# Row statistics of two tiles on ScalarE, one load for two tiles, an uneven split of the last tile and a reordered list in a fused attention and MLP kernel

## The chip, the cores and the metric

The kernel runs on one core of a Trainium2 chip. The time is device microseconds of one execution; a run of the kernel before took 220.25 us (median of 3, 219.59 to 220.25). Besides the times there is one profiled execution, from which all rows come.

## The reference

x has 2048 rows of 512 values in bf16. The result is the sum of x, an attention branch and an MLP branch, both fed by the layer norm of x:

```
xn = layernorm(x)                                    # over 512 columns, no scale or bias
q, k, v = xn @ wq, xn @ wk, xn @ wv                  # 32 heads of 16, 4 segments of 512 rows
for each segment s:
    p     = softmax(causal(q k^T / 4));  a_dot = p v
    a_mem = phi(q) M / (phi(q) z + 1e-6)             # phi(t) = t + 1 if t > 0 else exp(t)
    o     = sigmoid(beta) a_mem + (1 - sigmoid(beta)) a_dot
    M += phi(k)^T v;  z += sum of phi(k)
out = x + o @ wo + silu(xn @ w1) @ w2                # w1: 512 x 1792, w2: 1792 x 512
```

## The kernel before, in words

The 2048 rows are 16 tiles of 128, four to a segment. The whole order of the work is written out by hand in the string ORDER (line 17). Each word of it is one small piece of work: a letter code that names a function in the dictionary PIECES (line 867), and numbers for segment, tile and part. The loop at line 904 calls the pieces in this order; each engine and each queue then executes its own instructions in the order in which they were issued, and waits where an operand is not ready.

The words that matter here:

- `xc` and `xd` (ln_sums, ln_var, lines 284 and 288) take one bn_stats and one bn_aggr of a tile of x on VectorE; `xs` is both. `xq` (ln_sqrt, line 302) takes the square root of variance plus eps on ScalarE, `xi` (line 305) the reciprocal on VectorE, and `Nv` (ln_norm, line 313) normalises the tile on VectorE. From tile 4 on, `xg` takes the roots of four tiles on GpSimd instead.
- `X` (turn_mm, line 840) transposes a normalised tile with four products on TensorE, and `Xa` or `Xv` (turn_copy, line 847) copies it out of PSUM on ScalarE, in two halves, or on VectorE. From tile 4 on `XD` transposes by a DMA on SP's queue.
- `k`, `q`, `v`, `h` are the dense products of a segment, in four parts per group in segments 0 and 1 (each part one product of 512 columns or two of 256); `kv`, `ka`, `qv`, `qa`, `vv` are the copies out of PSUM, on VectorE or ScalarE; `kf` and `kp` split k for the scores; `ha` and `hv` are the tanh and the product of silu; `fa`, `fp`, `fv`, `ga` are pieces of phi; `tb` is a one-element exponential that brings its table in early; `tanh` is one small ScalarE step; `lw` loads w2 or wo on ScalarE's queue.
- `S` (scores, line 707) is one of 72 batches of scores: 8 or 16 small products into the one psS tile, which takes four PSUM banks (psatt, bufs=1), and one exponential over 128x2048 on ScalarE; GpSimd then masks it. `E` and `O` weigh v with them. The batches run in the list's order S0, S2, S1, S3, S4, S7, S5, S11, S6, S8, S9, S10, S13 and on to S71.
- `o`, `oc`, `od` (out_mm, line 628) are output products with all, half or a quarter of the 512 columns; `oh` (half_out, line 660) is the same for the last tile, which is made in two halves of 256 columns, h = 0 and 1. `st` (lines 616 and 674) evicts and stores a tile, `sh` (half_store, line 663) a half of the last one. Outputs of the last segment's tiles 2 and 3 lie in the banks of the psS tile.
- `busy` (line 861) issues products on zeros whose result nobody reads, 44 and then 6 at the start.

The four loads of the first tiles of x are issued at lines 163 to 166, tiles 0 and 2 on SP's queue, 1 and 3 on ScalarE's; SP then issues the weights wv, wk, wq, further x, and w1.

Late in the list TensorE's products are issued as four narrow ones of 32 output rows each (product, line 333), side by side in the array.

Of the kernel before, what the change touches and what calls it, by code (L numbers as in the profile page):

```python
# [8 lines left out]
AF = mybir.ActivationFunctionType  # L9
# [5 lines left out]

ORDER = """
ones0 ones1 zeros xc0 xd0 xc1 xq0 xi0 Nv0 busy44 xd1 xq1 xc2 busy6 xi1 X0.1 xd2 xq2 Nv1 X1.1 Xa0.1 v0.0.0 v0.0.1 v0.0.2 xs3 xi2 Nv2 xq3 xi3 v0.0.3 X2.1 Xa1.1 k0.1.0 tb Nv3 X3.1 Xv2.1 k0.1.1 Xv3.1 vv0.0 odd omask k0.0.0 k0.0.1 k0.0.2 k0.0.3 ka0.0 fp0.0 q0.0.0 kf0.0 q0.0.1 q0.0.2 q0.0.3 k0.1.2 k0.1.3 q0.2.0 v0.2.0 qa0.0 xs5 ka0.1 kp0.1
S0 v0.1.0 v0.1.1 xs6 xs7 q0.2.1 v0.2.1 v0.2.2 v0.2.3 vv0.2 fa0.0 k0.2.0 k0.2.1 k0.2.2 xs4 xg4.4
S2 q0.2.2 q0.2.3 qv0.2 k0.2.3 kv0.2 fa0.2 v0.1.2 v0.1.3 vv0.1 Nv5 Nv6 XD6 q0.1.0 q0.1.1 q0.1.2 q0.1.3 Nv7 qv0.1
S1 h0.0.0 h0.0.1 h0.0.2 fp0.2 xs10 h0.0.3 v0.3.0 v0.3.1 v0.3.2 v0.3.3 ha0.0 vv0.3 q0.3.0 hv0.0  # L20
S3 h0.3.0 h0.3.1 q0.3.1 kp0.2 q0.3.2 h0.3.2 tanh XD5 XD7 q0.3.3 h0.3.3 k0.3.0 qv0.3 k0.3.1 xs8 ha0.3
S4 Nv4 h0.1.0 k0.3.2 h0.1.1 hv0.3 XD4 h0.2.0 h0.2.1 h0.2.2 h0.2.3 ha0.2 xs9 k0.3.3 kv0.3 hv0.2
S7 xs11 xg8.4 v1.2.0 v1.2.1 v1.2.2 v1.2.3 vv1.2 h0.1.2 h0.1.3 ha0.1 E0
S5 h0.4.0 h0.4.1 hv0.1 Ev0 h0.4.2 h0.4.3 v1.1.0 v1.1.1 fv0.2 v1.1.2 v1.3.0 fp0.3 ha0.4 v1.1.3 vv1.1
S11 hv0.4 q1.2.0 q1.2.1 q1.2.2 v1.3.1 kind fa0.1 q1.2.3 qv1.2 v1.3.2 v1.3.3 vv1.3 Nv8 XD8 O0 lw0 fv0.0 Ov0
S6 fa0.3 k1.2.0 k1.2.1 k1.2.2 h0.5.0 h0.5.1 h0.5.2 q1.1.0 h0.5.3 ha0.5 kp0.3 k1.2.3 kv1.2 q1.1.1 q1.1.2 hv0.5
S8 h0.7.0 q1.1.3 qv1.1 h0.6.0 h0.6.1 h0.6.2 h0.6.3 ha0.6 kp1.2 fv0.3 E1 Ev1 k1.0.0
S9 hv0.6 h0.7.1 h0.7.2 h0.7.3 Om0 ha0.7 k1.0.1 k1.0.2 q1.0.0 q1.0.1 fp0.1 Nv9 XD9 k1.0.3 q1.0.2 kv1.0 kp1.0
S10 h0.8.0 hv0.7 xs12 h0.8.1 h0.8.2 h0.8.3 ha0.8 h0.9.0 h0.9.1 q1.0.3 t0.3 qv1.0 Nv10 XD10 h0.9.2 h0.9.3
S13 hv0.8 O1 Ov1 xs15 v1.0.0 v1.0.1 v1.0.2 ha0.9 v1.0.3 vv1.0 h0.10.0 h0.10.1 bmask  # L30
# [63 lines left out]
def kernel(  # L94
# [207 lines left out]
    def ln_sqrt(t):  # L302
        nc.scalar.activation(out=rstd_all[:, t, :], in_=mv_all[:, t, 1:2], func=AF.Sqrt, bias=eps[:, 0:1])

# [8 lines left out]
    def ln_norm(t, eng):  # L313
        xn[t] = work.tile([P, D], BF16, name="xn_t", tag="x_res", bufs=4)
        eng.tensor_scalar(  # L315
            out=xn[t][:], in0=xs(t, t + 1)[:, 0, :], scalar1=mv_all[:, t, 0:1], scalar2=rstd_all[:, t, 0:1],
            op0=ALU.subtract, op1=ALU.mult,
        )
# [344 lines left out]
    def half_store(h):  # L663

        st, j, cols = sts[LAST], TPS - 1, slice(h * D // 2, (h + 1) * D // 2)
        assert len(st.pop(("done", j, h))) == 4 * (FT + DT)
        o_half = work.tile([P, L], BF16, name="o_half", tag="pos")[:, 0 : D // 2]
        out = nc.vector.scalar_tensor_tensor(
            out=o_half, in0=st["psO", j, h], scalar=0.5, in1=st["x", j][:, cols], op0=ALU.mult, op1=ALU.add
        )  # L670
        fin_out.append(((j, h), out))
        nc.sync.dma_start(out=out_flat[(NT - 1) * P : NT * P, cols], in_=o_half)
# [188 lines left out]
    def keep_busy(n):  # L861
# [81 lines left out]
```

## Time and profile before

| | us |
|---|---|
| median of 3 runs | 220.25 |
| profiled execution | 219.92 |
| its span | 218.2 |
| TensorE busy | 210.5 |
| ScalarE busy | 184.2 |
| VectorE busy | 179.0 |
| GpSimd busy | 126.8 |

The span is counted from the first to the last event of the profiled execution; times such as 7.17 are microseconds from its start. In the rows, PE is TensorE (PEld its weight loads), ACT ScalarE, DVE VectorE, POOL GpSimd, SP the SyncE queue. A row of the order in time has the start, the time until the last instruction of the group ends, the engine, the source line, the operation, output <- input, and the count. A row of the table by stretches has the stretch, its length, the busy time and instruction count of PE, PEld, DVE, ACT and POOL, the clock granted to TensorE, the DMA share and GB/s. A row of the chain of waits has start, length, engine, output, source line and count.

### The profile page before, as it was taken

How to read it: one execution, taken by the hardware profiler on the slowest of the kernel's cores; microseconds unless marked ns; L12 is line 12 of the kernel's file. 1: busy time of each engine (PE TensorE's matmuls, PEld its weight loads, DVE VectorE, ACT ScalarE, POOL GpSimd, SP SyncE). 2: the span in 40 equal slices, each digit the busy share in tenths (PEclk: the TensorE clock that was granted, in tenths of full speed). 3: DMA queues.
4: the chain of work that ended last, by engine and by line, in shares of the span. 5: the costliest groups of instructions: out<-in, count | busy, mean ns of one | idle time of the engine just before them, and what ended most of it. 6: DMA issues, size and time to landing. Idle time of an engine off the chain costs nothing.

```text
span 218.2 us, 9261 instructions
## 1 busy us (share of the span) xinstructions
PE 210.5 (96%) x3979; PEld 115.0 (53%) x4003; DVE 179.0 (82%) x370; ACT 184.2 (84%) x173; POOL 126.8 (58%) x203
## 2 busy tenths in 40 slices
PE   7899999999999999999999999999999999999994
PEld 7566656655644544444444545445454544465663
DVE  5899999999799879557989886887878897868753
ACT  3799999999999999999999999999989998942000
POOL 6066868969568973886766436963786373410000
PEclk9999999999999999999999999999999999999999
DMA  5995348322203222442125131420042120412322
GB/s 179 357 373 152 51 110 258 62 66 53 51 5 99 75 63 39 99 79 52 49 70 81 54 96 28 74 74 9 0 131 76 48 75 13 133 34 80 91 77 75
DMA packets 33273, 19.60 MB, mean 90 GB/s; under 512 B 14672, under 2 KB 33232, under 8 KB 33232
## 3 DMA queue, kind: packets, MB, share of 16 engines
q1 hardware_dynamic: 30608, 16.39, 28.7%
q10 hardware_dynamic: 2624, 2.62, 3.8%
q8 instruction: 31, 0.51, 1.0%
q14 instruction: 10, 0.08, 0.1%
HBM read 9.96 MB, written 2.10 MB: 55 GB/s over the span
## 4 chain that ended last, share of the span: by engine, by line
PE 92%; DVE 2%; ACT 2%; DMA 1%; issue 1%
PE ps L336 26%; PE psO L338 16%; PE ps L338 16%; PE psS L724 11%; PE psO L336 9%; PE psV L791 8%; PE psS L338 4%; ACT Pb L730 2%; DMA x_lo<-in_A_x_dram 1%; DVE stats L286 1%; PE psM L452 1%; PE ptr L845 0%; DVE xn_t L315 0%; PE ps L509 0%; DVE odd L828 0%
## 5 line engine op out<-in xcount | busy, mean ns | idle before, releaser
L730 ACT ACTIVATE Pb<-psS 128x2048 bf16<-128x2048 f32 x72 | 135.2, 1878 | 4.5 <-PE psS L724 2.2
L744 POOL TENSOR_SCALAR_AFFINE_SELECT Pb<-Pb 128x512 bf16<-128x512 bf16 (+2 forms) x88 | 62.1, 715 | 22.1 <-ACT Pb L730 19.2
L497 DVE SCALAR_TENSOR_TENSOR hT<-th,ps 128x512 bf16<-128x512 bf16 x56 | 38.0, 682 | 11.0 <-ACT th L492 10.6
L744 POOL TENSOR_SCALAR_AFFINE_SELECT lows<-Pb 64x512 bf16<-64x512 bf16 (+1 forms) x40 | 22.9, 572 | 32.5 <-ACT Pb L730 24.2
L338 PE MATMUL psO<-w_sb,hT 128*32 128x512 bf16 (+2 forms) x692 | 41.0, 320 | 0.0
L336 PE MATMUL ps<-xnT,w_sb 128*128 128x512 bf16 (+1 forms) x177 | 36.1, 330 | 0.4 <-DVE pk L433 0.2
L492 ACT ACTIVATE th<-ps 128x512 bf16<-128x512 f32 x56 | 33.0, 593 | 3.7 <-PE ps L338 3.3
L338 PEld LDWEIGHTS <-hT 128*32 128x32 bf16 x860 | 21.4, 96 | 14.5 <-issue 3.1
L338 PE MATMUL ps<-xnT,w_sb 128*32 128x512 bf16 (+1 forms) x408 | 24.6, 349 | 0.0
L724 PE MATMUL psS<-qT,k 32*128 32x64 bf16 (+3 forms) x512 | 23.0, 233 | 0.2
L336 PEld LDWEIGHTS <-w_sb 128*128 128x128 bf16 x178 | 16.4, 98 | 12.0 <-issue 1.2
L336 PE MATMUL psO<-w_sb,hT 128*128 128x512 bf16 (+2 forms) x83 | 20.6, 325 | 0.6 <-issue 0.5
L791 PEld LDWEIGHTS <-Vz 128*32 128x32 bf16 x768 | 16.0, 97 | 9.5 <-issue 0.6
L791 PE MATMUL psV<-Pb,Vz 128*32 128x448 bf16 (+7 forms) x512 | 20.9, 286 | 0.0
L724 PEld LDWEIGHTS <-k 32*128 32x128 bf16 x512 | 9.3, 92 | 21.5 <-issue 20.3
L724 PE MATMUL psS<-qT,kT 16*128 16x448 bf16 (+3 forms) x256 | 14.7, 269 | 0.0
L336 PE MATMUL ps<-xnT,wk_sb 128*128 128x256 bf16 (+1 forms) x63 | 14.1, 326 | 0.2
L336 PEld LDWEIGHTS <-hT 128*128 128x128 bf16 x93 | 8.5, 98 | 9.7 <-issue 2.1
L338 PEld LDWEIGHTS <-w_sb 128*32 128x32 bf16 x408 | 9.9, 96 | 6.6 <-issue 1.5
L828 DVE CAST odd<-psV 128x512 bf16<-128x512 f32 x16 | 11.0, 686 | 2.6 <-PE psV L791 2.4
L399 DVE CAST qT<-ps 128x512 bf16<-128x512 f32 x15 | 10.3, 687 | 3.4 <-PE ps L336 1.8
L338 PE MATMUL psO<-wo_sb,oT 128*32 128x512 bf16 x140 | 12.8, 380 | 0.0
(112 smaller groups left out, 326.7 us busy)
## 6 DMA issues: line engine op xcount, KB each, us to landing
spr<-rz SPq DMA_DIRECT2D x56, 64.0 KB
x_res<-in_A_x_dram SPq DMA_DIRECT2D x16, 128.0 KB
out_dram<-o_out SPq DMA_DIRECT2D x15, 128.0 KB
w_sb<-in_B_w_dram SPq DMA_DIRECT2D x2, 896.0 KB
w_sb<-in_B_w_dram ACTq DMA_DIRECT2D x1, 1792.0 KB
x_hi<-in_A_x_dram SPq DMA_DIRECT2D x2, 512.0 KB
wv_sb<-in_A_wv_dram SPq DMA_DIRECT2D x2, 256.0 KB
wk_sb<-in_A_wk_dram SPq DMA_DIRECT2D x1, 512.0 KB
```

The lines of the kernel that those rows point to most:

```text
L286: nc.vector.bn_stats(out=stats[t][:], in_=xs(t, t + 1)[:, 0, :])
L336: return [nc.tensor.matmul(out, lhsT=lhsT, rhs=rhs, start=start, stop=stop, skip_group_check=True)]
L338: nc.tensor.matmul(out[c : c + 32], lhsT=lhsT[:, c : c + 32], rhs=rhs, start=start, stop=stop, tile_position=(0, c), skip_group_check=True,)
L399: copy(out=seg_tile(s, "qT")[:, dt, :], in_=sts[s].pop(("q", dt))[:, :])
L452: nc.tensor.matmul(psM[32 * g : 32 * g + 32, i, :].rearrange("p (r d) -> p r d", d=DH), lhsT=st["phiK", dt][:, j, 32 * g : 32 * g + 32], r ...
L492: nc.scalar.activation(out=th[:], in_=sts[s]["h", ft][:, :], func=AF.Tanh, scale=0.5)
L497: nc.vector.scalar_tensor_tensor(out=st["hT"][:, ft, :], in0=st.pop(("th", ft))[:], scalar=1.0, in1=st.pop(("h", ft))[:, :], op0=ALU.add, ...
L724: nc.tensor.matmul(psS[:, g, c : c + q2 - q1], lhsT=keys[rows], rhs=st["qT"][rows, dt, q1:q2], start=True, stop=True, tile_position=(32 * ...
L730: exp = nc.scalar.activation(out=blocks(Pb, b).rearrange("p y g c -> p g y c"), in_=psS[:, :, :].rearrange("p g (y c) -> p g y c", c=BLOCK ...
L744: over[id(Pb)].append(nc.gpsimd.affine_select(out=out, in_=in_, compare_op=ALU.is_ge, fill=0.0, base=base, pattern=[[0, out.shape[1]], [1, ...
L791: nc.tensor.matmul(psV[32 * g : 32 * g + 32, q0 : q0 + nq].rearrange("p (y c) -> p y c", y=weights.shape[2]), lhsT=Vzs[s % 2][:, kt, 4 * d ...
L828: copy(out=odd[:], in_=sts[s].pop(("psV", 1))[:, :])
```

## The change

Five things change.

1. Tiles 1 and 3 of x get their sums on ScalarE: `xa` takes the negative mean (Copy with scale -1/512 and accumulation), `xb` the sum of the squared deviations (Square with the negative mean as bias, and accumulation). The root then scales by 1/512 and the normalisation adds instead of subtracting. `xc1`, `xd1` and `xs3` go.
2. x's tiles 2 and 3 come in one load of 256 KB on ScalarE's queue, behind tile 1's; SP has one load fewer.
3. The idle products are 40 in one row instead of 44 and 6.
4. The turned tiles 0 and 1 are copied by VectorE in one piece each (`Xv`) instead of by ScalarE in two.
5. The last tile is made in parts of 128 (h = 0, stored last) and 384 columns (h = 1). The list is reordered: from the start to S10, in one word around S68 and S66, and in the last line.

```diff
-    load_x(nc.sync, 2, 1)
-    load_x(nc.scalar, 3, 1)
+    load_x(nc.scalar, 2, 2)
...
+    def ln_mean_act(t):
+        by_act.add(t)
+        nc.scalar.activation(
+            out=work.tile([P, D], BF16, name="junk", tag="ex")[:], in_=xs(t, t + 1)[:, 0, :],
+            func=AF.Copy, scale=-1.0 / D, accum_out=mv_all[:, t, 0:1],
+        )
+
+    def ln_square_act(t):
+        nc.scalar.activation(
+            out=work.tile([P, D], BF16, name="junk", tag="ex")[:], in_=xs(t, t + 1)[:, 0, :],
+            func=AF.Square, bias=mv_all[:, t, 0:1], accum_out=mv_all[:, t, 1:2],
+        )
...
-        width = D if half is None else D // 2
-        first = 0 if half is None else half * width
+        first, width = (0, D) if half is None else LAST_COLS[half]
...
+    LAST_COLS = [(0, P), (P, D - P)]
...
-        st, j, cols = sts[LAST], TPS - 1, slice(h * D // 2, (h + 1) * D // 2)
+        (first, width), st, j = LAST_COLS[h], sts[LAST], TPS - 1
+        cols = slice(first, first + width)
...
-        ptr, parts = xn.pop(("ptr", t)), 2 if t < 2 else 1
+        ptr, parts = xn.pop(("ptr", t)), 2 if t < 2 and copy is act else 1
```

The old list up to S3 and from S11 to S8 (lines 17 to 21 and 25 to 27):

```
ones0 ones1 zeros xc0 xd0 xc1 xq0 xi0 Nv0 busy44 xd1 xq1 xc2 busy6 xi1 X0.1 xd2 xq2 Nv1 X1.1 Xa0.1 v0.0.0 v0.0.1 v0.0.2 xs3 xi2 Nv2 xq3 xi3 v0.0.3 X2.1 Xa1.1 k0.1.0 tb Nv3 X3.1 Xv2.1 k0.1.1 Xv3.1 vv0.0 odd omask k0.0.0 k0.0.1 k0.0.2 k0.0.3 ka0.0 fp0.0 q0.0.0 kf0.0 q0.0.1 q0.0.2 q0.0.3 k0.1.2 k0.1.3 q0.2.0 v0.2.0 qa0.0 xs5 ka0.1 kp0.1
S0 v0.1.0 v0.1.1 xs6 xs7 q0.2.1 v0.2.1 v0.2.2 v0.2.3 vv0.2 fa0.0 k0.2.0 k0.2.1 k0.2.2 xs4 xg4.4
S2 q0.2.2 q0.2.3 qv0.2 k0.2.3 kv0.2 fa0.2 v0.1.2 v0.1.3 vv0.1 Nv5 Nv6 XD6 q0.1.0 q0.1.1 q0.1.2 q0.1.3 Nv7 qv0.1
S1 h0.0.0 h0.0.1 h0.0.2 fp0.2 xs10 h0.0.3 v0.3.0 v0.3.1 v0.3.2 v0.3.3 ha0.0 vv0.3 q0.3.0 hv0.0
S3 h0.3.0 h0.3.1 q0.3.1 kp0.2 q0.3.2 h0.3.2 tanh XD5 XD7 q0.3.3 h0.3.3 k0.3.0 qv0.3 k0.3.1 xs8 ha0.3
...
S11 hv0.4 q1.2.0 q1.2.1 q1.2.2 v1.3.1 kind fa0.1 q1.2.3 qv1.2 v1.3.2 v1.3.3 vv1.3 Nv8 XD8 O0 lw0 fv0.0 Ov0
S6 fa0.3 k1.2.0 k1.2.1 k1.2.2 h0.5.0 h0.5.1 h0.5.2 q1.1.0 h0.5.3 ha0.5 kp0.3 k1.2.3 kv1.2 q1.1.1 q1.1.2 hv0.5
S8 h0.7.0 q1.1.3 qv1.1 h0.6.0 h0.6.1 h0.6.2 h0.6.3 ha0.6 kp1.2 fv0.3 E1 Ev1 k1.0.0
...
```

The new list up to S10:

```
ones0 ones1 zeros busy40 xc0 xd0 xa1 xq0 xi0 Nv0 xb1 xq1 X0.1 xc2 xi1 xd2 Nv1 X1.1 Xv0.1 v0.0.0 v0.0.1 xa3 xq2 v0.0.2 xb3 v0.0.3 xi2 Xv1.1 Nv2 v0.1.0 xq3 xi3 Nv3 X2.1 v0.1.1 X3.1 Xv2.1 Xv3.1 v0.1.2 v0.1.3 k0.0.0 k0.0.1 k0.0.2 vv0.1 k0.0.3 odd tb vv0.0 k0.1.0 q0.0.0 q0.0.1 omask ka0.0 q0.0.2 kf0.0 q0.0.3 k0.1.1 xs7 xs6 k0.1.2 k0.1.3 qa0.0 ka0.1 xs5 k0.2.0 xs4 xg4.4
S0 k0.2.1 v0.2.0 v0.2.1 fa0.0 v0.2.2 q0.1.0 q0.1.1 q0.1.2 q0.1.3 q0.2.0 qv0.1
S2 k0.2.2 k0.2.3 q0.2.1 q0.2.2 q0.2.3 h0.0.0 kv0.2 v0.2.3 fa0.2 h0.0.1 qv0.2 kp0.1 vv0.2
S1 q0.3.0 q0.3.1 q0.3.2 q0.3.3 h0.0.2 v0.3.0 Nv6 qv0.3 Nv7 h0.0.3 fp0.2 Nv5 ha0.0 h0.3.0
S3 h0.3.1 hv0.0 h0.3.2 v0.3.1 h0.3.3 h0.2.0 h0.2.1 v0.3.2 XD6 XD5 ha0.3 xs9 xs10 h0.2.2
S4 v1.2.0 hv0.3 v0.3.3 h0.2.3 v1.2.1 Nv4 ha0.2 vv0.3 xs11 v1.2.2 XD7 hv0.2 v1.2.3 k0.3.0 fp0.0 XD4 k0.3.1 k0.3.2
S7 h0.1.0 kp0.2 h0.1.1 vv1.2 k0.3.3 h0.1.2 h0.1.3 E0 ha0.1 kv0.3 h0.4.0 Ev0
S5 v1.1.0 v1.1.1 v1.1.2 h0.4.1 xs8 v1.1.3 hv0.1 h0.4.2 fv0.2 h0.4.3 tanh ha0.4 xg8.4 vv1.1 fp0.3 v1.3.0 v1.3.1
S11 hv0.4 fa0.1 v1.3.2 q1.2.0 q1.2.1 q1.2.2 v1.3.3 O0 kind vv1.3 q1.2.3 h0.5.0
S6 qv1.2 Ov0 h0.5.1 h0.5.2 k1.2.0 k1.2.1 k1.2.2 Nv8 k1.2.3 q1.1.0 kp0.3 h0.5.3 Nv9 ha0.5 kv1.2 q1.1.1
S8 q1.1.2 q1.1.3 h0.6.0 h0.6.1 hv0.5 qv1.1 h0.7.0 h0.6.2 h0.6.3 ha0.6 E1 fv0.0 fa0.3 kp1.2 Ev1 k1.0.0
S9 fp0.1 XD9 h0.7.1 h0.7.2 k1.0.1 fv0.3 hv0.6 q1.0.0 Om0 k1.0.2 q1.0.1 h0.7.3 ha0.7 k1.0.3 kv1.0 q1.0.2 Nv10 hv0.7 XD8
S10 t0.3 XD10 xs12 h0.9.0 h0.9.1 h0.9.2 h0.8.0 q1.0.3 kp1.0 h0.8.1 h0.8.2 qv1.0 h0.8.3 h0.9.3 ha0.8 lw0
```

The end of the last line, before and after (what comes ahead has other oh words in other places, but the same work; `od2.2.13.0` moves from S66 to S68):

```
before: st3.0 o3.1.17 st3.2 oc3.1.10.0 oh17.1 oh14.1 oh15.1 o3.1.16 o3.1.13 oh2.1 oh1.1 sh1
        o3.1.8 oh17.0 oh16.0 st3.1 oh13.0 oh6.0 oh2.0 oh1.0 oh3.0 oh14.0 sh0
after:  st3.0 oc3.1.10.1 o3.1.17 st3.2 oc3.1.10.0 oh17.1 o3.1.16 o3.1.13 o3.1.8 o3.1.15 st3.1
        oh14.1 oh15.1 oh2.1 oh16.1 oh1.1 sh1 oh15.0 oh4.0 oh10.0 oh17.0 oh16.0 oh13.0 oh6.0
        oh2.0 oh1.0 oh3.0 oh14.0 sh0
```

More of the change, by code (lines that the diff above doesn't have):

```diff
@@ L13 @@
 I32 = mybir.dt.int32
[L16 to L29, printed above, removed]
+ORDER = """ones0 ones1 zeros busy40 xc0 xd0 xa1 xq0 xi0 Nv0 xb1 xq1 X0.1 xc2 xi1 xd2 Nv1 X1.1 Xv0.1 v0.0.0 v0.0.1 xa3 xq2 v0.0.2 xb3 v0.0.3 xi2 Xv1.1 Nv2 v0.1.0 xq3 xi3 Nv3 X2.1 v0.1.1 X3.1 Xv2.1 Xv3.1 v0.1.2 v0.1.3 k0.0.0 k0.0.1 k0.0.2 vv0.1 k0.0.3 odd tb vv0.0 k0.1.0 q0.0.0 q0.0.1 omask ka0.0 q0.0.2 kf0.0 q0.0.3 k0.1.1 xs7 xs6 k0.1.2 k0.1.3 qa0.0 ka0.1 xs5 k0.2.0 xs4 xg4.4
@@ L316, in ln_norm @@
             out=xn[t][:], in0=xs(t, t + 1)[:, 0, :], scalar1=mv_all[:, t, 0:1], scalar2=rstd_all[:, t, 0:1],
-            op0=ALU.subtract, op1=ALU.mult,
+            op0=ALU.add if t in by_act else ALU.subtract, op1=ALU.mult,
         )
```

16 lines of the change are left out of this document (10 added, 6 removed).

## The prediction, made before the changed kernel ran

> **What bounds the kernel now.** The page comes first: its span, its busy shares and the shares of the chain that ended last. Then a table by stretches, from the first exponential of the scores (12.36 us) to the fourteenth batch, S13's (41.76), from there to the last one's stretch (190.0), and from there to the last product.
>
> ```profile
> span 218.2 us, 9261 instructions
> ...
> PE 92%; DVE 2%; ACT 2%; DMA 1%; issue 1%
> ...
> 12.36:41.76 29.40, 29.00 (x441) 18.43 (x448) 28.39 (x62) 28.98 (x26) 22.03 (x35) 1.00 0.59 163
> 41.76:190.00 148.24, 146.22 (x2814) 73.12 (x2824) 123.86 (x248) 143.53 (x126) 99.30 (x151) 1.00 0.26 62
> 190.00:215.30 25.30, 25.19 (x632) 15.45 (x624) 17.18 (x34) 4.43 (x6) 1.24 (x3) 1.00 0.24 71
> ```
>
> TensorE carries 92% of the chain, at a granted clock of 1.00 in all three stretches. But in the first one ScalarE is just as full (28.98 of 29.40 us, TensorE 29.00). Since matmul ends are modelled, the order in time has to say who waits there. These are ScalarE's exponentials of S0, S2, S4, S11, S6, S8 and S13, and from the chain of waits the scores of S7:
>
> ```profile
> 12.36 1.88 ACT L730 ACTIVATE Pb<-psS 128x2048 bf16<-128x2048 f32 x1
> 14.75 1.88 ACT L730 ACTIVATE Pb<-psS 128x2048 bf16<-128x2048 f32 x1
> 21.96 1.88 ACT L730 ACTIVATE Pb<-psS 128x2048 bf16<-128x2048 f32 x1
> 29.10 1.88 ACT L730 ACTIVATE Pb<-psS 128x2048 bf16<-128x2048 f32 x1
> 31.62 1.88 ACT L730 ACTIVATE Pb<-psS 128x2048 bf16<-128x2048 f32 x1
> 34.44 1.88 ACT L730 ACTIVATE Pb<-psS 128x2048 bf16<-128x2048 f32 x1
> 41.76 1.88 ACT L730 ACTIVATE Pb<-psS 128x2048 bf16<-128x2048 f32 x1
> 23.89 0.40 PE psS L724 x8
> ```
>
> The scores of S7 start at 23.89, that is 0.05 us after S4's exponential ends (21.96 + 1.88 = 23.84): there is one psS tile (four banks), so the next scores cannot start before the exponential has read the last ones. While TensorE makes them, ScalarE does one other 0.6 us step, and the beat is 14.75 - 12.36 = 2.39 us, about as much as TensorE's words of one batch take. So from 12.36 to 41.76 ScalarE sets the beat, and **the time at which S0's exponential starts decides when S13's does**. After S13 both lists hold the same words up to two spots near the end, so what is late at S13 is late at the end.
>
> The other two places are the start, where the layer norm of x's first tiles leads up to S0, and the tail behind the last product (three stores, an evicting VectorE step of 0.42 us, the way to DRAM). The profiled execution took 219.92 us, which is 1.72 more than its span; the median is 220.25. I work with differences and add them to both.
>
> **The start.** The rows of the start in order of time:
>
> ```profile
> 3.64 0.69 DVE L286 BATCH_NORM_STATS2 stats<-x_lo 128x6 f32<-128x512 bf16 x1 [1.01 <-DMA x_lo<-in_A_x_dram]
> 4.65 0.29 ACT L303 ACTIVATE rstd_all<-mv_all,eps 128x1 f32<-128x1 f32 x1 [1.44 <-DVE mv_all L289]
> 5.23 0.41 DVE L315 TENSOR_SCALAR xn_t<-x_lo,mv_all,rstd_all 128x512 bf16<-128x512 bf16 x1
> 5.55 0.17 DVE L289 BATCH_NORM_AGGREGATE mv_all<-stats 128x2 f32<-128x6 f32 x1
> 5.65 0.66 DVE L286 BATCH_NORM_STATS2 stats<-x_lo 128x6 f32<-128x512 bf16 x1
> 6.22 0.14 DVE L306 RECIPROCAL rstd_all<-rstd_all 128x1 f32<-128x1 f32 x1
> 6.44 0.38 DVE L315 TENSOR_SCALAR xn_t<-x_lo,mv_all,rstd_all 128x512 bf16<-128x512 bf16 x1
> 6.73 0.69 DVE L286 BATCH_NORM_STATS2 stats<-x_lo 128x6 f32<-128x512 bf16 x1
> 7.17 1.04 PE L336 MATMUL ps<-wv_sb,xnT 128*128 128x512 bf16 x3
> 8.19 0.40 PE L845 MATMUL ptr<-ident,xn_t 128*128 128x128 bf16 x4
> 8.43 0.38 PE L336 MATMUL ps<-xnT,wk_sb 128*128 128x256 bf16 x2
> 8.52 1.28 ACT L309 ACT_TABLE_LOAD   x1
> 8.63 0.94 DVE L851 COPY xnT<-ptr 128x512 bf16<-128x512 bf16 x2
> 11.91 0.21 PE L724 MATMUL psS<-qT,k 32*128 32x64 bf16 x4
> 14.13 0.62 ACT L423 ACTIVATE ex<-kT 128x512 bf16<-128x512 bf16 x1
> 138.63 0.86 PE ps L336 x4
> ```
>
> Removed from VectorE: two sums with their aggregates (xc1 xd1 and xs3), 2 x (0.69 + 0.17) = 1.7 us. Added: the copies of X0 and X1, 2 x 0.47 = 0.9 us by the row at 8.63. ScalarE gets four passes over 128x512 and loses its copies. No row shows a pass that also sums: it costs 0.62 us (the exponential at 14.13) and, for the accumulator and a bias, between nothing and the 0.29 us of the square root's row; I take 0.15, because the bare root, nearly all of it start-up, is the far end. ScalarE is idle for 1.44 us before the first root, so tile 1's mean (3.65 to about 4.4) ends before tile 0's variance is there at about 4.6; the root stays at 4.65 and the first normalise at 5.23. The squares then run from 4.9 to about 5.7, tile 1's root to 6.0, and the reciprocal's turn on VectorE comes later than that, so these four passes cost nothing; if that cover goes, each 0.1 us costs 0.1 us.
>
> On VectorE xd1 (5.55 to 5.65) is gone, so tile 2's sums start at 5.55, the reciprocal at 6.12, Nv1 at 6.34, and it ends at 6.72. Now Xv0.1 follows on VectorE instead of ScalarE: 6.72 to 7.19, so the first v product starts at 7.24 instead of 7.17. Behind it TensorE has v0.0 and v0.1.0 while VectorE makes Xv1.1 (7.7), Nv2 (8.1) and Nv3 (8.5); X2 and X3 fit in, and the short stall between the row at 7.17 and X2's at 8.19 goes. From there I see no stall up to S0. The first exponential table (1.28 us) loads at about 7.9 and is off the path, as before.
>
> But the new list puts 21 four-per-group words (v0.0, v0.1, k0.0, k0.1, q0.0 and k0.2.0) ahead of S0, the old one 18. Price of a word: before, X2 (0.24 by the rows at 8.19 and 8.43), X3 and 14 words lie between 8.19 and 11.91, (3.72 - 0.48) / 14 = 0.231 us with its small stalls; undisturbed it is 0.86 / 4 = 0.215 (the row at 138.63). Scores of S0: 7.24 + 0.48 + 21 words = 12.23 to 12.57; I take 12.4, between the two. The exponential followed 0.45 later (12.36 - 11.91) and would start at 12.85: **0.5 us later than now (0.3 to 0.65)**. TensorE is ahead by three words then, but loses them at S2, S1 and S3, which have 8 words for 9 in the old list, and waits for the exponentials instead.
>
> From S0 to S13 the ScalarE steps are the same ones, with tanh and fa0.3 moved. Of the 29.40 us, 0.42 were ScalarE's idle time. S11 to S6 took 2.52 us where the beat is 2.39, and S6 to S8 2.82 with two extra steps and 11 words on TensorE; the new list has 9 words there. Some 0.26 of the 0.42 should come back (bounds: nothing, all). So S13 stands **0.24 us later** (0.5 - 0.26; bounds 0.3 - 0.42 = -0.12 and +0.65).
>
> The other moves at the start I cost at nothing. SP issues one load fewer ahead of the weights, but the bytes ahead of them are the same. The joint load of x's tiles 2 and 3 stands second on ScalarE's queue; what if it is late is a rival below. XD6 stands behind Nv6 on SP's queue as before, but v1.2.0, its first reader, comes one batch sooner; I take a wait there as unlikely, since Nv6 comes in S1 and v1.2.0 only behind S4's scores. Two row groups speak for the idle products:
>
> ```profile
> 1.10:2.20 1.10, 1.09 (x11) 1.10 (x12) 0.80 (x1) 0.48 (x1) 0.96 (x7) 1.00 0.13 40
> 4.40:5.50 1.10, 0.99 (x18) 0.82 (x15) 1.06 (x4) 0.29 (x1) 0.00 (x0) 1.00 0.84 241
> ```
>
> They come at 0.10 us each first and at 0.055 to 0.06 at the end, while the clock column says 1.00 throughout. Ten fewer end about 0.6 us sooner, at 4.8, with nothing behind them that waits.
>
> **The tail.** Evictions of the last tile, their stores, and the DMA traffic after the last product (last two columns: DMA share, GB/s):
>
> ```profile
> 214.16 0.42 DVE L668 SCALAR_TENSOR_TENSOR o_half<-psS,x_res 128x256 bf16<-128x256 f32 x1 [0.83 <-PE psS L338]
> 214.50 0.68 DVE L621 SCALAR_TENSOR_TENSOR o_out<-psO,x_res 128x512 bf16<-128x512 f32 x1
> 215.25 0.42 DVE L668 SCALAR_TENSOR_TENSOR o_half<-psS,x_res 128x256 bf16<-128x256 f32 x1
> 215.70 0.33 SPq L672 DMA_DIRECT2D out_dram<-o_half  x1
> 214.32 0.90 PE psS L338 x32
> 216.50:216.75 0.25, 0.00 (x0) 0.00 (x0) 0.00 (x0) 0.00 (x0) 0.00 (x0) 1.00 0.70 205
> 216.75:217.00 0.25, 0.00 (x0) 0.00 (x0) 0.00 (x0) 0.00 (x0) 0.00 (x0) 1.00 0.23 62
> 131.55 0.55 PE psV L791 x32
> 214.80 0.11 PEld L338 LDWEIGHTS <-oT 128*32 128x32 bf16 x4
> ```
>
> 256 columns cost VectorE 0.42 us and 512 cost 0.68, so 128 cost about 0.29: 0.13 us less behind the last product. Eleven narrow parts stand behind sh1's last product; eight groups of 256 columns take 0.90, 0.11 each, so 128 columns take 0.056 and eleven 0.62 us, in which sh1's 384 columns (0.55 by the same line) are evicted. SP then issues the two stores back to back (0.33 each), the last at about 215.57 against 215.70. The last 64 KB flowed from 216.5 (0.80 after the issue) to about 216.8; 32 KB from 216.37 take 0.13 us at that rate, or 0.26 if rows half as long go at half the rate. Together 0.19 to 0.32 us less; I take **-0.25**, the middle. If sh1 ends late after all, the last step waits, by up to 0.3 us: upper bound +0.1.
>
> The columns multiplied are as many as before. Narrow parts would still cost more if TensorE were bound by its weight loads: a group of four takes 0.11 us (the row at 214.80). The row at 131.55 speaks against it: 32 products in eight groups, each with weights of its own, in 0.55 us, 0.069 a group, half of them 64 columns wide. The Trainium skill, "TensorE: Matmul & The Clock Gate", section LDWEIGHTS, gives a load as its columns / 1.2 ns: by that, as an estimate, four loads of 32 columns take 0.107 us one after the other, and the 18 narrow parts would be bound by them. The trace does not agree with such loads in a row: by that rule eight groups could not pass in 0.55 us.
>
> Sum: +0.24 - 0.25 = about 0. On the profiled 219.92 that is 219.9, on the median **220.2 us**; with the bounds -0.12 - 0.32 = -0.44 and +0.65 + 0.1 = +0.75.
>
> **The rivals.**
>
> *TensorE sets the beat, not ScalarE (faster).* Then the later S0 costs nothing: TensorE's stream starts where it did (7.24, against 11.91 - 0.48 - 18 x 0.231 = 7.27), and the 0.40 us that it idles from 12.36 to 41.76 can be filled from the three words in hand: -0.03 - 0.40 - 0.32 = -0.75, 219.5. For it: 29.00 of 29.40 us busy. Against it: the scores at 23.89 start as soon as the exponential lets them.
>
> *The joint load is late (slower).* Tile 2's sums stand ahead of tile 1's reciprocal, Nv1 and Xv0.1 on VectorE. Before, they started at 5.65 and tile 3's at 6.73, both without a wait on a load, so the trace bounds tile 3's landing by 6.73 only. The joint load is complete when both tiles are; from 5.55 on each 0.1 us delays the first product, S0 and the end by as much, at most by 1.18: 0.24 + 1.18 - 0.25 = +1.17, 221.4. For it: tile 2 now shares a queue behind tile 1, with the weights beside it. Against it: tile 0, first on its queue as tile 1 is on the other, was summed from 3.64 on. The same page of the skill, Part 1, says that an idle stretch of some 3.4 us halves TensorE's clock; the idle products end at 4.8, so a first product past 8.2 would pay for that as well, which no row here shows.
>
> *The narrow parts are bound by their weight loads (slower).* 18 x (0.11 - 0.056) = 0.97 us on top: 0.24 + 0.97 - 0.25 = +0.96, 221.2.
>
> *The squares need another table (slower).* Between the roots, each Square would bring loads of 1.28 us in and back, two on tile 1's way: over 2 us, 222.5. The copies at L851 ran between the roots without one; no row shows a Square.
>
> **How the numbers follow.** Forecast 0.55; TensorE's beat 0.19; late load 0.19; weight loads 0.04; tables 0.03. A measurement of this kernel can tell about 0.3%, 0.66 us, from no change. The forecast's own range, 219.8 to 221.0, lies nearly all within that; its upper end is past it, for which I move 0.02 to slower, and 0.01 of the rival at 219.5 falls inside. Faster 0.18, same 0.54, slower 0.28. The range reaches down to 219.5 and up to 221.3, which leaves out the tables and the last of the late load.
>
> **What would show it.** The changed profile should have the first v product at 7.2 to 7.3 and no gap before X2; the scores of S0 at 12.2 to 12.6 and the exponential at 12.65 to 13.0; S13's exponential at 41.6 to 42.4, with the 2.4 us beat between; a last eviction of about 0.29 us and 0.2 to 0.3 us less from last product to end. A bn_stats row that waits for the x_lo load, a third table load, narrow groups at 0.11 us, or S13 ahead of 41.6 would each prove one part wrong.

## The result and the profile after

The changed kernel takes **222.69 us** (median of 6 executions, 221.85 to 225.76) against 220.25 for the kernel before (219.59 to 220.82, 6 executions), a ratio of 1.0111 (95% interval 1.0085 to 1.0137). It is slower by 2.4 us, outside the range that was given. The profiled execution took 221.85 us with a span of 220.1, against 219.92 and 218.2. In ten of the 80 executions, here and below, of kernels with the sums on ScalarE and 40 idle products, and in none of the others, the mean granted clock is 0.992 and the time some 2 to 3 us longer (in these six the one of 225.76 us, which the ratio leaves out); what brings that stays open.

The time is lost in one place. Both lists name the same 72 batches, and each batch has one large exponential on ScalarE, so the lateness can be read batch by batch: start of the n-th exponential after, minus that before.

| exponential | before | after | later by |
|---|---|---|---|
| 1st (S0) | 12.36 | 12.62 | 0.26 |
| 13th (S13) | 41.76 | 41.91 | 0.15 |
| 16th | 48.94 | 49.08 | 0.14 |
| 17th (S21) | 51.36 | 53.51 | 2.15 |
| 72nd (S71, the last) | 190.26 | 192.40 | 2.14 |
| end of the span | 218.2 | 220.1 | 1.9 |

Up to the 16th, and from the 17th to the last, nothing changes by more than some tenths. Between the two lie 2 us. First ScalarE's rows in the order of time of the kernel after, with the load of w2 (the second MLP weight) that stands on its queue:

```profile
12.62 1.88 ACT L747 ACTIVATE Pb<-psS 128x2048 bf16<-128x2048 f32 x1
...
41.40 0.42 ACTq L167 DMA_DIRECT2D w_sb<-in_B_w_dram  x1
...
49.08 1.88 ACT L747 ACTIVATE Pb<-psS 128x2048 bf16<-128x2048 f32 x1
50.86 0.59 ACT L508 ACTIVATE th<-ps 128x512 bf16<-128x512 f32 x1
53.51 1.88 ACT L747 ACTIVATE Pb<-psS 128x2048 bf16<-128x2048 f32 x1 [2.06 <-PE psS L741]
```

ScalarE waits 2.06 us for scores. Why they are late is in the waits of the kernel after from 46 to 55 us (columns: who, for whom, us in total, times, longest):

```profile
ACT Pb L747 <- PE psS L741: 2.1, 1, 2.1
PEld L468 <- DMA phiK<-pk: 1.9, 1, 1.9
PE psM L468 <- DMA phiK<-pk: 1.6, 1, 1.6
DVE M L480 <- PE psM L468: 1.2, 1, 1.2
```

and in its chain of waits from 41 to 54 us:

```profile
44.80 7.65 DMA phiK<-pk
52.45 0.04 issue
52.49 0.38 PE psM L468 x32
52.87 0.25 PE ps L354 x8
53.12 0.33 PE psS L741 x8
```

TensorE executes its list in order. The 32 products psM of the word `m0.2`, which stand in S17's line, need phiK turned by the DMA transpose `t0.2`. That transpose was issued at 44.80 and its reader got on 7.65 us later. Everything behind it on TensorE, the scores of S21 too, waited. The same places in the order of time of the kernel before:

```profile
29.11 0.39 ACTq L169 DMA_DIRECT2D w_sb<-in_B_w_dram  x1
...
44.54 1.19 SPq L441 DMA_TRANSPOSE phiK<-pk  x1
...
50.34 0.40 PE L452 MATMUL psM<-Vz,phiK 128*32 128x32 bf16 x32
...
51.36 1.88 ACT L730 ACTIVATE Pb<-psS 128x2048 bf16<-128x2048 f32 x1
```

Here the transpose was issued at almost the same time (44.54), and 5.8 us later the products found it done, without a wait in their row. What differs is the load of w2: issued at 29.11 before, at 41.40 after. In the list that is the word `lw0`, which stood behind `O0` in S11 and now stands last in S10, 12 us later. It moves 1792 KB, and from 41.40 on these bytes flow while SP's queue brings the transposes. The DMA queues of the kernel after (q10 carries the w2 load, q1 SP's queue, q14 instructions; packets, MB, share of 16 engines), in the stretches 43 to 47, 49 to 50.5 and 50.5 to 52 us:

```profile
q10 hardware_dynamic: 1147, 1.17, 96.6%
q14 instruction: 2, 0.02, 1.6%
q1 hardware_dynamic: 54, 0.01, 1.1%
...
q10 hardware_dynamic: 391, 0.39, 74.0%
q1 hardware_dynamic: 486, 0.12, 35.4%
...
q1 hardware_dynamic: 717, 0.27, 121.2%
q10 hardware_dynamic: 27, 0.02, 4.4%
```

and of the kernel before from 45.5 to 47.5 us:

```profile
q1 hardware_dynamic: 634, 0.22, 51.4%
```

and, from 43 to 47 us, of e1, the first experiment below, which has the new list with the load of w2 back in its old place:

```profile
q1 hardware_dynamic: 1106, 0.27, 34.6%
```

Before, the transpose's bytes (and those of x_res behind it) were through some 3 us after its issue. After, SP's queue moved 54 packets from 43 to 47 us and the load 1147. That SP's queue had work in that time e1 shows: there it issues the same transfers within 0.3 us of the same times and moves 1106 packets. SP's queue comes to 0.27 MB in 1.5 us only when the load has run dry. The Trainium skill, "DMA: Bandwidth & Descriptors", section Queues, rings and completion order, says that each DMA engine takes turns between the queues that it has work for, packet by packet. This trace does not look like even turns from 43 to 47 us, but it does from 49 to 50, where both queues move 265 packets. What holds SP's queue back in the first stretch, no run here shows.

### The profile page after: what moved, and what is told of

The parts are those of the page before. It is cut to its first block, busy times and chain, and to the rows that moved or that the text cites. A ratio compares the mean times of both kernels' runs of the same rounds, so it can differ in the third digit from the quotient of the medians.

```text
span 220.1 us, 9275 instructions
## 1 busy us (share of the span) xinstructions
PE 211.4 (96%) x3987; PEld 114.8 (52%) x4011; DVE 178.3 (81%) x368; ACT 185.9 (84%) x177; POOL 125.7 (57%) x203
## 4 chain that ended last, share of the span: by engine, by line
PE 80%; ACT 6%; DMA 5%; DVE 5%; issue 2%; SPq 0%; DVEq 0%; ACTq 0%
PE ps L352 21%; PE psO L354 16%; PE ps L354 13%; PE psS L741 9%; PE psO L352 9%; PE psV L808 7%; ACT Pb L747 4%; PE psS L354 4%; DMA phiK<-pk 3%; DMA x_lo<-in_A_x_dram 1%; DVE stats L284 1%; DVE hT L513 1%; ACT th L508 1%; PE psM L468 1%; ACT ex L439 1%
## 5 line engine op out<-in xcount | busy, mean ns | idle before, releaser
L354 PEld LDWEIGHTS <-hT 128*32 128x32 bf16 x860 | 20.9, 97 | 14.9 <-issue 3.1
L354 PE MATMUL ps<-xnT,w_sb 128*32 128x512 bf16 (+1 forms) x440 | 26.0, 343 | 0.0
L352 PEld LDWEIGHTS <-w_sb 128*128 128x128 bf16 x170 | 15.7, 98 | 12.8 <-issue 1.0
L354 PEld LDWEIGHTS <-w_sb 128*32 128x32 bf16 x440 | 11.0, 97 | 6.5 <-issue 1.5
L352 PE MATMUL ps<-xnT,wk_sb 128*128 128x512 bf16 (+1 forms) x61 | 13.2, 328 | 0.2
```

What stands on the lines that cost most here:

```text
L352: return [nc.tensor.matmul(out, lhsT=lhsT, rhs=rhs, start=start, stop=stop, skip_group_check=True)]
L354: nc.tensor.matmul(out[c : c + 32], lhsT=lhsT[:, c : c + 32], rhs=rhs, start=start, stop=stop, tile_position=(0, c), skip_group_check=True,)
```

## The experiments

Two theories stood at first. **A**: the moved load of w2 holds up the transpose, and nothing else in the change matters by more than some tenths. **B**: the transposes hold up one another, since the new list issues XD8 to XD10, `t0.3` and `t0.2` closer together, and would do so without the load. All ratios are to the kernel before, run beside each kernel on the same chip.

**The load back in its place (e1).** The changed kernel, with `lw0` where it was.

```diff
-S11 hv0.4 fa0.1 v1.3.2 q1.2.0 q1.2.1 q1.2.2 v1.3.3 O0 kind vv1.3 q1.2.3 h0.5.0
+S11 hv0.4 fa0.1 v1.3.2 q1.2.0 q1.2.1 q1.2.2 v1.3.3 O0 lw0 kind vv1.3 q1.2.3 h0.5.0
-S10 ... h0.9.3 ha0.8 lw0
+S10 ... h0.9.3 ha0.8
```

> The changed kernel with one word moved: lw0, the load of w2 on ScalarE's queue, goes back from the end of S10 to its old place behind O0 in S11. Theory A (the load of w2, issued at 41.40 us instead of 29.11, holds up the DMA transpose of phiK that was issued at 44.80, and TensorE waits for it at 52.49): the wait goes, the exponentials from S21 on stand 0.1 to 0.3 us behind those of the kernel before instead of 2.14, the span is 218.0 to 218.4 and the ratio to the kernel before 0.998 to 1.002. Theory B (the reordered transposes XD8, XD9, XD10 and t0.3 hold each other up on SP's queue, with or without the load): the wait stays, span about 220.1, ratio 1.008 to 1.012.

Measured: 220.23 us against 220.06, ratio 1.0026 (1.0001 to 1.0051), span 218.4. In its order of time:

```profile
29.33 0.37 ACTq L167 DMA_DIRECT2D w_sb<-in_B_w_dram  x1
...
51.51 1.88 ACT L747 ACTIVATE Pb<-psS 128x2048 bf16<-128x2048 f32 x1
```

The 17th exponential is 0.15 us later than before, not 2.15, with no wait in its row. B falls: the transposes stand as close as in the changed kernel and are in time. From the 28th exponential on e1 is 0.4 us late; the last section says why.

**The load moved alone (e2).** The kernel before, with nothing changed but `lw0`, from S11 to the end of S10.

```diff
-S11 ... Nv8 XD8 O0 lw0 fv0.0 Ov0
+S11 ... Nv8 XD8 O0 fv0.0 Ov0
-S10 ... Nv10 XD10 h0.9.2 h0.9.3
+S10 ... Nv10 XD10 h0.9.2 h0.9.3 lw0
```

> The kernel before with one word moved: lw0 from S11 to the end of S10, where the change has it. Theory A: the transpose of phiK issued at about 44.5 lands past 51 and TensorE waits for it, +1.5 to +2.5 us, ratio 1.007 to 1.012. Theory B: its transposes stand as before, so nothing changes, ratio within 0.002 of 1.

Measured: 222.15 us, ratio 1.0096 (1.0068 to 1.0124), span 220.0. The exponentials are within 0.02 us of those before up to the 16th, and 1.77 later from the 17th to the end. From its waits:

```profile
PEld L452 <- DMA phiK<-pk: 1.8, 1, 1.8
ACT Pb L730 <- PE psS L724: 1.8, 1, 1.8
```

One word of the list makes the loss by itself, in the old kernel as in the new.

**The reader later (e3).** The changed kernel with the load late, and `m0.2 mv0.2` moved from S17's line to the end of S16's, so that the transpose has more time.

```diff
-S17 ... h0.12.1 xs14 m0.2 mv0.2 ha1.10 h0.12.2
+S17 ... h0.12.1 xs14 ha1.10 h0.12.2
-S16 ... q2.1.1 qv2.1 E3
+S16 ... q2.1.1 qv2.1 m0.2 mv0.2 E3
```

> The changed kernel with lw0 left at the end of S10, but m0.2 mv0.2, the products that read the late transpose, moved from S17 to the end of S16, three batches (some 7 us) later. If the late transpose costs only because TensorE's order stands behind its reader (theory A as I state it), the 2 us go and the ratio is 0.998 to 1.003, though the transpose still lands at about 52.4. If the load delays more than that (the moves of the sums, x's transposes, other loads), a wait shows up in another place and 1 us or more stays: ratio over 1.004.

Measured: 221.33 us, ratio 1.006 (1.0039 to 1.0081), span 219.4. The 17th exponential is back at +0.11, so the 2 us at that place are gone, but from the 20th on there is a new loss of 1.0. In the order of time:

```profile
57.66 0.42 PE L468 MATMUL psM<-Vz,phiK 128*32 128x32 bf16 x32
58.63 0.73 PE L808 MATMUL psV<-Pb,Vz 128*32 128x512 bf16 x16 [0.56 <-DVE qT L415]
```

The move itself made that: behind psM in its new place TensorE waits for VectorE. By its ratio the run lands where the expectation put a load that delays more than this transpose; the trace shows no wait for a transpose from 46 to 62 us. So the run speaks for A, but it is no repair.

**The transpose earlier (e7, e11).** The changed kernel with the load late. In e7 `t0.2` is issued in S9, ahead of XD9, and so ahead of the load. In e11 the other transpose of phiK, `t0.3`, also goes from S10 into S9.

```diff
-S9 fp0.1 XD9 h0.7.1 h0.7.2 k1.0.1 fv0.3 hv0.6 ...
+S9 fp0.1 t0.2 XD9 h0.7.1 h0.7.2 k1.0.1 fv0.3 t0.3 hv0.6 ...        (t0.3: e11 alone)
-S10 t0.3 XD10 xs12 ...
+S10 XD10 xs12 ...                                                  (e11 alone)
-S12 k1.1.0 k1.1.1 k1.1.2 t0.2 k1.1.3 ...
+S12 k1.1.0 k1.1.1 k1.1.2 k1.1.3 ...
```

> The changed kernel with lw0 left at the end of S10 and its reader left in S17, but the late transpose itself, t0.2, issued ahead of XD9 at the start of S9, before the load of w2. Its input is ready by S5. Theory A (this one transpose behind this one load): TensorE's wait of 2 us goes without any other move, S21's exponential stands 0.1 to 0.4 us behind the kernel before, ratio 1.000 to 1.004. If the load holds up more than that one transpose (XD10, XD11, the moves of the sums), another wait appears before 60 us and the ratio stays over 1.005.

Measured (e7): 221.61 us, ratio 1.0067 (1.0041 to 1.0092), span 219.6. Its chain of waits:

```profile
42.00 9.77 DMA phiK<-pk
51.77 0.04 issue
51.81 0.28 PE psM L468 x16
```

Now `t0.2` is in time and `t0.3`, issued at 42.00, is late instead: it took 9.77 us to its reader, the second half of the same 32 products, and the 17th exponential stands at +1.34.

> The changed kernel with the load of w2 left at the end of S10, and both transposes of phiK (those of batches 2 and 3) issued in S9 ahead of the load of x's tile. If the wait of 2 us is that of a transpose which is issued behind the load of w2, it is gone, S21's exponential stands +0.1 to +0.4 us against the kernel before in place of +2.15, and the ratio is 1.000 to 1.004. If the load also delays what was issued ahead of it, or the next load of x, a wait of 0.8 us or more is left between 45 and 58 us, and the ratio is above 1.005.

Measured (e11): median 220.72 us, ratio 1.0042 (1.0016 to 1.0068); one of the ten executions took 734.86 us, which the ratio leaves out and for which nothing here gives a cause. The profiled one took 219.88 with a span of 218.2, that of the kernel before to the tenth:

```profile
41.42 0.42 ACTq L167 DMA_DIRECT2D w_sb<-in_B_w_dram  x1
...
51.52 1.88 ACT L747 ACTIVATE Pb<-psS 128x2048 bf16<-128x2048 f32 x1
```

With the load as late as in the changed kernel, the 17th exponential stands at +0.16. So the wait in the profile hangs on one thing: whether a transpose that TensorE needs soon is issued ahead of the load or behind it. The median is 0.84 above the profiled execution, and without a trace of the others it stays open what they pay.

**The tail (e4, e5).** e4 is the kernel before with the parts of 128 and 384 columns and the new last line, and nothing else. e5 is e1 with the old halves and the old last line.

```diff
-    LAST_COLS = [(0, P), (P, D - P)]
+    LAST_COLS = [(0, D // 2), (D // 2, D // 2)]       (e5, with the last line of the kernel before)
```

> The kernel before with the tail of the change alone: the last tile in parts of 128 and 384 columns and the new last line of the list. By the prediction's working the time from the last product to the end falls by 0.19 to 0.32 us and nothing else moves: ratio 0.9985 to 0.9995. If the narrow parts are bound by their weight loads: +0.7 us, ratio 1.003. If the rows of 256 bytes cost as much as they save: no change from last product to end beyond the 0.13 us of the shorter eviction.

> The changed kernel with lw0 back in S11 (as in the first experiment) and the tail undone: halves of 256 columns and the old last line. What is left of the change is the start (sums on ScalarE, joint load, 40 idle products, copies on VectorE) and the lists up to S10. If the tail gives what it gave in the profiles so far (0.1 to 0.25 us), this is slower than the first experiment by that: S13 0.15 us behind the kernel before, span 218.3 to 218.7, ratio 1.000 to 1.003. If the start is worth more than S13's place says (TensorE sets the beat), the span is below 218.2 and the ratio below 0.999.

Measured: e4 220.12 us, ratio 0.9996 (0.9981 to 1.001); e5 220.36, ratio 1.0018 (0.9992 to 1.0045). By the time nothing can be told. From the last exponential to the end of the span e1 takes 0.22 us less than before and e4 0.11 less, but so does e5 with the old tail, so these three traces alone do not settle it. All of them together do: that stretch is 0.20 to 0.23 us shorter in ten of the thirteen traces with the new tail and 0.11 or 0.12 in the other three (e4, e6, e12); with the old tail it is 0.01, 0.02 and 0.11 shorter (e2, e13, e5). e4's profiled execution is late from the start for another reason, in TensorE's order of time:

```profile
9.15 0.39 PE L336 MATMUL ps<-xnT,wk_sb 128*128 128x256 bf16 x2 [0.86 <-DMA wk_sb<-in_A_wk_dram]
```

The first weights wk came 0.86 us late, and all 72 exponentials stand 0.66 to 0.74 later. That code was not touched by the edit, so this is what the start's loads can do in a single execution.

**The loads of x apart (e6), and S0 sooner (e8).** e6 is e1 with x's tiles 2 and 3 in two loads again. e8 is e1 with three words less ahead of S0 (`v0.1.2 v0.1.3 vv0.1` go behind q0.0) and `lw0` in S7.

```diff
-    load_x(nc.scalar, 2, 2)                           (e6)
+    load_x(nc.sync, 2, 1)
+    load_x(nc.scalar, 3, 1)
```

> The changed kernel with lw0 back in S11 and x's tiles 2 and 3 loaded apart again, tile 2 on SP's queue and tile 3 on ScalarE's. Tile 2's sums started at 5.44 us in the changed kernel without a wait on the joint load, so I expect no difference: first exponential at 12.6 to 12.7, ratio to the kernel before as in the first experiment, 1.000 to 1.004. If the joint load spares SP's queue something that matters, the weights come later and the first exponential with them, by 0.2 us or more.

> A version meant to beat both: the changed kernel with lw0 in S7, where no transpose is under way, and two words of the start moved: v0.1.2 v0.1.3 with their copy vv0.1 behind q0.0 instead of ahead of k0.0. In the changed kernel S0's first exponential waited for the chain k0.0, ka0.0, kf0.0, qa0.0 on ScalarE; k0.0 comes two words (0.43 us) sooner, but its second half needs Xv3.1 (9.43 us), so I expect the first exponential at 12.3 to 12.5 instead of 12.62, S13 level with the kernel before or up to 0.15 us ahead, with the tail 0.2 us less: span 217.8 to 218.1, ratio 0.997 to 1.000. If the first exponential is bound by something else it stays at 12.6 and the ratio is that of the first experiment.

Measured: e6 220.15 us, ratio 0.9999 (0.9979 to 1.002); e8 221.19, ratio 1.0045 (1.0018 to 1.0072). e8 missed: its first exponential is 1.13 us later than before, not sooner. VectorE's order of time in e8, and behind it the same step in the changed kernel:

```profile
5.99 0.69 DVE L284 BATCH_NORM_STATS2 stats<-x_lo 128x6 f32<-128x512 bf16 x1 [0.58 <-DMA x_lo<-in_A_x_dram]
```

```profile
5.44 0.69 DVE L284 BATCH_NORM_STATS2 stats<-x_lo 128x6 f32<-128x512 bf16 x1
```

In e8's profiled execution the joint load came late. It is issued before anything that e8 edits, so this is the late load that the prediction had as a rival, seen in one execution and not in the others that were traced. But the late load is not all of it: the first v product starts 0.56 us later than in the changed kernel (7.61 against 7.05), and from there to the scores of S0 e8 takes 5.43 us (to 13.04) where the changed kernel takes 5.12 (to 12.17), so in this execution the new order is itself slower by 0.31. And 1.0026 for e1 against 0.9999 for e6 is a difference inside their intervals.

**The idle products (e9, e10, e13, e14, e15).** e1 with 50, 20, 60 and 45 idle products (`busy40` replaced), and the kernel before with 40 (`busy44` replaced by `busy34`).

> The same kernel with 20 idle products. If their number decides whether the granted clock falls back in the first stretches, more runs than with 40 show a mean of 0.992 and 2 us more, or the whole start runs slower and the ratio is 1.004 to 1.012. If their number has nothing to do with it, the ratio is that of the kernel with 40, 1.001 to 1.003, and about one run in nine shows 0.992.

> The changed kernel with the load of w2 back in S11 behind the product O0, and 50 idle products in place of the 40. If the idle products only fill time in which TensorE has nothing to do, the first exponential comes where it came with 40 (+0.26 us against the kernel before, give or take 0.1) and the ratio is 1.001 to 1.003 as with 40. If the ten products that were taken away keep the granted clock up, no run shows a mean granted clock of 0.992 (8 of about 70 runs of the kernels with 40 did), no run stands 2 us above the others, and the ratio is at the lower end, 1.000 to 1.002. If the ten products stand in the way of the scores, the first exponential is later by up to 1.0 us (ten at 0.10 us).

> The changed kernel with the load of w2 back in S11, and 60 idle products. If the wait at 51 us that the kernels with 50 show (0.9 us, not in those with 40) comes with more idle products as such, it is there with 60 too, and the ratio is 1.003 or more. If it hangs on where the pages of TensorE's instructions fall (20 instructions further on with each ten products), it may be gone, the ratio 1.000 to 1.002, or the first exponential is late by what the products beyond 50 take (ten at 0.1 us, 1.0 us at most, ratio up to 1.005).

> The same with 45 idle products. If more idle products as such bring the wait at 51 us, half of it or more is there (ratio 1.002 to 1.004). If it hangs on the place of a page, it is there whole or not at all. If the count holds the clock, no execution shows a mean clock of 0.992.

> The kernel before with 40 idle products in place of 50 (34 and 6), nothing else changed. As the prediction costed it, at nothing: ratio 0.998 to 1.002 and the first exponential within 0.1 us of that of the kernel before. If the ten products hold TensorE's speed up in its first products, the first exponential is later by 0.5 us or more, or some executions stand 2 us above the others, and the ratio is above 1.002.

| kernel | idle products | median us | ratio (interval) | first exponential |
|---|---|---|---|---|
| e10 | 20 | 222.22 | 1.0109 (1.0085 to 1.0132) | +1.99 |
| e1 | 40 | 220.23 | 1.0026 (1.0001 to 1.0051) | +0.26 |
| e15 | 45 | 220.11 | 1.0004 (0.9989 to 1.002) | +0.15 |
| e9 | 50 | 220.87 | 1.0038 (1.0026 to 1.005) | +0.12 |
| e14 | 60 | 221.65 | 1.0069 (1.0055 to 1.0083) | +0.98 |
| e13, kernel before | 40 | 220.58 | 1.0023 (1.0007 to 1.0039) | +0.22 |

With 20 TensorE stands still from 3.4 us on. Its order of time in e10, then in the changed kernel:

```profile
5.62 0.61 PE L862 MATMUL ptr<-ident,xn_t 128*128 128x128 bf16 x4 [2.20 <-DVE xn_t L331]
...
7.17 2.34 PE L352 MATMUL ps<-wv_sb,xnT 128*128 128x512 bf16 x5
9.30 0.63 PE L862 MATMUL ptr<-ident,xn_t 128*128 128x128 bf16 x4
```

```profile
5.58 0.61 PE L862 MATMUL ptr<-ident,xn_t 128*128 128x128 bf16 x4
6.72 0.40 PE L862 MATMUL ptr<-ident,xn_t 128*128 128x128 bf16 x4 [0.53 <-DVE xn_t L331]
7.05 1.25 PE L352 MATMUL ps<-wv_sb,xnT 128*128 128x512 bf16 x4
```

Five v products take 2.34 us, four take 1.25: in e10 a product comes every 0.43 us (7.17 to 9.30, five), in the changed kernel every 0.27 (7.05 to the next turn at 8.14, four). Undisturbed it is 0.215 (the prediction's row at 138.63), half of e10's. The clock column of the table by stretches says 1.00 for both, but it counts the time ahead of a trace's first record of the granted clock as full. That record, at full clock, starts at 10.46 us in e10. With 40 to 60 idle products, in either kernel, it starts between 3.92 us (the kernel before) and 6.74 (e2), and with the same 40 at 4.62 in e7 and at 6.66 in e11 (e3 and e8 hold no record). So the idle products do buy speed: at 20 the first products run at half speed; at 60 the last ten, at 0.1 us each, stand in the way; between 40 and 50 the traces do not tell the counts apart at the start. The Trainium skill, "TensorE: Matmul & The Clock Gate", Part 1, gives half the clock until about 3.4 us of work have gone by, and adds that the window runs free, so that the same kernel warms up at different points. The traces agree: with the same 40 idle products the first turn (four ptr products at 5.58) takes 0.61 us in the changed kernel, whose record starts at 6.15, and 0.40 in e1, whose record starts at 4.88.

Two things here did not come out clear. e13's 0.22 us is no matter of the clock: its first v product starts at 7.11, 0.06 sooner than before, and then TensorE waits 0.18 us for wk's load. And e9 shows a wait of 0.93 us in front of the 17th exponential that neither 45 nor 60 shows:

```profile
52.23 1.88 ACT L747 ACTIVATE Pb<-psS 128x2048 bf16<-128x2048 f32 x1 [0.93 <-PE psS L741]
```

By the records the scores it waits for start at 50.92. So it does not follow the count, and what brings it stays open.

**What the runs speak for (e12).** e6 with 50 idle products: load of w2 early, x's tiles in two loads, sums on ScalarE, narrow last part.

> What the runs speak for: the load of w2 in S11 behind O0, x's tiles 2 and 3 in two loads, 50 idle products, the sums on ScalarE and the narrower last tile. Start +0.15 to +0.25 us against the kernel before, end -0.13 to -0.24, so a ratio of 0.998 to 1.001 and no wait above 0.5 us that the kernel before does not have. If the idle products or the two loads cost anything at the start, the first exponential is beyond +0.5 us and the ratio above 1.002.

Measured: 220.8 us, ratio 1.0036 (1.0022 to 1.005), a miss: first exponential +0.33, and the same wait as e9's (0.92 us) in front of the 17th. The best of the changed kernels, e6 (ratio 0.9999) and e15 (1.0004), cannot be told from the kernel before.

## Why the prediction was wrong

**The step that failed** is "The other moves at the start I cost at nothing". `lw0` moved by 12 us in the very list that the step was about, and the prediction neither named nor costed it; and "After S13 both lists hold the same words up to two spots near the end, so what is late at S13 is late at the end" took the words for the work. The words after S13 were the same, but a transfer issued ahead of S13 reached into them: 1792 KB at 0.33 MB/us (0.65 MB in 2 us) are, as an estimate, 5.5 us of traffic at the least (the trace has its packets from 42 to 51 us), which lies across the transposes of 42 to 45 us and not, as before, across a stretch in which only XD8 was under way. e1 and e2 show this from both sides (2.0 and 1.77 us by the exponentials). What was needed stood in the trace of before: the transfers in flight between the load's new place and the next reader of each.

The other steps, one by one (S13 is the 13th batch, not the fourteenth as the prediction counts; its times are right):

- **S0 later by 0.5 us (0.3 to 0.65)**: measured 0.26, just under the bound. The price of the words was right; the first v product came at 7.05, not 7.24, because tile 2's sums started at 5.44 (5.55 was taken), and the exponential followed the scores (12.17) by 0.45, as taken.
- **S13 later by 0.24 (-0.12 to +0.65)**: measured 0.15. What comes back between S0 and S13 is 0.11 rather than 0.26; it and the miss at S0 partly cancel, so that the sum came out near is in part luck. That S0 decides when S13 starts is shown: in the twelve other traces of the changed kernel S0 is 0.12 to 1.99 us late, and S13 follows it with 0.11 or 0.12 less each time.
- **The four passes on ScalarE at nothing**: right, with one surprise. In ScalarE's order of time in the changed kernel:

```profile
4.78 0.71 ACT L316 ACTIVATE junk<-x_lo,mv_all 128x512 bf16<-128x512 bf16 x1
5.39 0.19 ACT L316 ACTIVATION_READ_ACCUMULATOR junk<-x_lo,mv_all 128x1 f32 x1
5.61 0.29 ACT L301 ACTIVATE rstd_all<-mv_all,eps 128x1 f32<-128x1 f32 x1
```

  The sum is read out by an instruction of its own. The step is 0.61 us from its start to that reading's start and some 0.2 more, about the 0.77 that was taken. Square between the roots brought no table load: the rival at 222.5 falls.
- **The tail, -0.25 (-0.32 to +0.1)**: measured -0.21 from the last exponential to the end (2.14 later there, 1.93 at the end by the times of the profiled executions). The last rows of the changed kernel:

```profile
216.77 0.91 DVE L685 SCALAR_TENSOR_TENSOR o_half<-psS,x_res 128x384 bf16<-128x384 f32 x2
216.83 0.45 PE L354 MATMUL psS<-w_sb,hT 128*32 128x128 bf16 x20
217.11 0.23 PE L354 MATMUL psS<-wo_sb,oT 128*32 128x128 bf16 x4
217.36 0.81 SPq L689 DMA_DIRECT2D out_dram<-o_half  x2
```

  Twenty narrow products, five groups, start within 0.28 us (216.83 to 217.11): 0.056 a group, as worked out. The rival of the weight loads (0.11) falls.
- **Forty idle products at nothing**: wrong in its reason. They were to end at 4.8; in the traced execution they took 0.1 us each to the last, and the first turn follows them at 5.58. They do not only fill time, they set the speed of the first products, as e10 shows. At 40 this cost nothing: in e1 they end sooner, and the first turn waits for xn_t and starts at 5.58 too.
- **TensorE sets the beat (219.5)**: falls, since S13 was late with S0. (Its sum takes the tail's far bound, 0.32, where the other rivals take 0.25; with that it is 219.6.) **The joint load is late (221.4)**: not in the traced execution of the changed kernel, but it was seen in e8, at the price that was given: tile 2's sums 0.55 us later than in the changed kernel (5.99 against 5.44) and the first v product 0.56.

What stays open: the median of the changed kernel is 0.84 us above its own profiled execution, and no trace of the other executions shows what they pay.

## What to carry to other kernels

A word of a schedule that issues a large DMA is not a detail of the word next to it: ask what else is in flight for as long as its bytes flow, above all small transfers that the bound engine needs next. Issue a bulk load where nothing small is waiting, or issue the small ones ahead of it (e11); a later reader (e3) or one early transpose of two (e7) left a wait in another place. When two lists are compared, compare the DMA issues by name and time first, and only then the compute words.

## What the runs showed of the hardware

- A bulk load of 1792 KB on ScalarE's queue all but stopped SP's queue, DMA transposes above all, for 4 us: 54 packets against the load's 1147 from 43 to 47 us, where e1 moves 1106 without the load. Two transposes took 7.65 and 9.77 us from issue to reader, where 5.8 had been enough with time to spare. Later, from 49 to 50 us, the two queues moved 265 packets each.
- Of two steps that VectorE and GpSimd start within 30 ns of each other, one took 0.6 to 0.9 us longer than it does in other traces. In e1, VectorE's step and then GpSimd's:

```profile
74.54 1.61 DVE L449 SCALAR_TENSOR_TENSOR phiQT<-ex,pos 128x512 bf16<-128x512 bf16 x1
```

```profile
74.51 1.09 POOL L761 TENSOR_SCALAR_AFFINE_SELECT Pb<-Pb 128x1024 bf16<-128x1024 bf16 x1
```

  In the kernel before the same two start at 74.38 and 74.37 and take 0.68 and 1.65: there GpSimd pays. In e1 VectorE pays, and the 28th exponential and all behind it stand 0.25 us later. So it is in all 17 traces: VectorE pays in eight, and each of these loses 0.24 or 0.25 us at the 28th exponential; GpSimd pays in the other nine, and none of them does. Very little decides it: e11 starts the two at 74.53 and 74.52, each 0.01 us off e1's, and there GpSimd pays.
- Ahead of a trace's first record of the granted clock TensorE is slow: in e10 v products start 0.43 us apart, with the record at 10.46 us, against 0.215 undisturbed; in the changed kernel the first turn takes 0.61 us, ahead of the record at 6.15, and the next, behind it, 0.40. The clock column reads 1.00 all the same, so in the first microseconds speed has to be read from durations.
